# g_norm spread by a small product, chunk 7 stored as halves from two queues, and a new order after chunk 1

## Chip, cores and metric

One core of one Trainium2 chip runs the whole program. The metric is the device time of one execution in microseconds; lower is better.

## What is computed

Two stages, float32 in and out. Linear attention without softmax, then an RMS norm with gains `g_norm`, gives `x` of 4608 rows by 512. A two-layer block with the SoLU activation and a layer norm follows.

```python
# q, k, v: (8, 8, 576, 64)
kv = einsum('bhsd,bhse->bhde', k, v)
o = einsum('bhsd,bhde->bhse', q, kv)
x = o / sqrt(mean(o * o, -1) + 1e-6) * g_norm      # g_norm: (64,)
x = x.transpose(0, 2, 1, 3).reshape(4608, 512)
h = x @ w_in                                       # (512, 1024)
sm = softmax(h)                                    # the sum has 1e-9 added
u = h * sm
ln = (u - mean(u)) / sqrt(var(u) + 1e-6) * g_ln
out = ln @ w_out                                   # (1024, 512)
```

## The kernel before

**Chunks.** The 4608 rows are worked in nine chunks of 512. Chunks 0 to 7 take 512 of the 576 rows of one batch each; chunk 8 takes the 64 rows left over in each of the eight batches (`q_last` gathers them). A name such as `h.5.2.1` is a step, a chunk, and one or two parts of the chunk.

**Steps of a chunk.** POOL issues the loads `q`, `k`, `v`, which cast to bf16. PE makes `kv_mm`; DVE or ACT copies it into `kvd` (steps `kv`). q is transposed, by PE (`qT_mm`, then a copy `qT`) up to chunk 4 and by a transposing DMA on SP (`qT`, line 425) in chunks 5 to 8. `o_mm` (lines 444 and 458) makes the attention output. Up to chunk 5 its norm runs `sq` (ACT squares), `s_mm` (PE, line 508), `ln` and `ex` (ACT, 512 and 516), and `x` (DVE, 528). In chunks 6 to 8 it runs `sq` (ACT), `ssum` (POOL, 473), `sred` (DVE, 478), `rh` (ACT, 484), `rg` (POOL, 489; reads `g_all`, the gains on every partition), `xt` (DVE, 496), and `x`, a transposing DMA on SP (line 500).

Then `h` (PE, lines 583 and 612) is 512 columns into one PSUM bank. Up to chunk 3 follow `exp` (ACT, 590), `u` (DVE, 594), `usq` (squares, mostly POOL, 238), `es` (POOL, 607) and the sums over all of them on PE (`sums`, 694) with `turn`, `stats` (DVE) and `rstd` (ACT). Chunks 4 to 8 have the rows on the partitions: `expt` (ACT, 620), `ut` (DVE, 626), `bn` (DVE statistics, 632), `stats` and `rstd`; and `turnu.c.half` (a transposing DMA on SP, line 648) turns half of `u` into `w`. Half 1 is the output tiles 2 and 3, half 0 the tiles 0 and 1.

`out` (PE, 760) multiplies with `w_out`; `ob` scales a finished tile by `rstd` out of PSUM (DVE 244 or ACT 242) into a buffer, and `store` (SP; in chunk 8 also ACT) writes it to HBM. In chunks 6 and 7 the rows of one tile go to two places in the output, so a store there is two DMAs of 64 partitions each (line 788). In chunk 8 the last tile is made, scaled and stored in two halves of its columns.

**What sets the order.** `ORDER` is written out by hand as a list of steps; the kernel emits them in that order, and each engine runs its own share of the list strictly in order. A step's suffix `:act` puts it on ACT where DVE would be the default (or POOL, for `usq` and `q_last`). `HOME` gives each PSUM tile one of eight banks, used one tile after another. `kept` says how many buffers of a kind there are; `q` has five, so the load of batch 6 waits for the last reader of batch 1, which is `q_last.1`. Semaphores keep what data and buffers require; `needs` in `add` only asserts that the list is in a possible order. A DMA on SP or ACT also waits for one issued eight DMAs earlier on the two. `FILL` puts idle products in front of some early PE steps.

`g_all` is loaded by one DMA on SP that repeats `g_norm` over 128 partitions (line 303). The gains are also among `g_rows` (nine rows of 128, the last one `g_norm` twice), which PE transposes early (`turn_g`) with the identity `eye`.

Of the kernel before, what the change touches and what calls it, by code (L numbers as in the profile page):

```python
# [39 lines left out]
kv.3.1.1:act kv.3.1.0 kv.3.0.2:act kv.3.1.2 ex.2.1.0 x.2.1.0 out.0.1.0 out.0.1.1 kv.3.0.0:act s_mm.2.1.1 ln.2.1.1  # L40
out.0.1.2 out.0.1.3 ob.0.1 usq.1.1 ex.2.1.1 h.2.7.0 x.2.1.1 qT_mm.3.0 qT.3.0:act h.2.5.0 q_last.3:act h.2.4.0 h.2.0.0
h.2.0.1 exp.2.0 q_last.1 h.2.3.0 h.2.6.0 h.2.3.1 exp.2.3 h.2.7.1 qT.3.1 u.2.0 kv_mm.5.0 kv.5.1.0 kv.5.0.1:act q.5.0
exp.2.7 kv.5.0.2:act kv.5.0.0:act h.2.4.1 exp.2.4 store.0.1 kv.5.1.1:act q.6.0 qT.5 u.2.3 u.2.7 kv.5.1.2 h.2.2.0
h.2.2.1 exp.2.2 usq.2.7 h.2.1.0 h.2.1.1 u.2.2 usq.2.0 h.2.6.1 u.2.4 o_mm.3.1 out.1.2.0 usq.2.2 out.1.2.1 exp.2.1
es.2.0 u.2.1 sq.3.1.0 exp.2.6 u.2.6 s_mm.3.1.0 ln.3.1.0 ex.3.1.0 sums.1 turn.1 stats.1 q_last.4 h.2.5.1 sq.3.1.1
out.1.3.0 q_last.2 g_all s_mm.3.1.1 kv_mm.4.0 exp.2.5 x.3.1.0 u.2.5 ln.3.1.1 es.2.1 usq.2.6 kv.4.0.0:act kv.4.0.2
kv.4.1.1 rstd.1 usq.2.5 ob.1.2 kv.4.0.1 ex.3.1.1 x.3.1.1 o_mm.3.0 sq.3.0.0 usq.2.4:act es.2.2 out.1.1.0 usq.2.1
kv.4.1.2:act out.1.3.1 ob.1.3 store.1.3 es.2.3 qT_mm.4.1 qT.4.1 sq.3.0.1 kv.4.1.0:act out.1.0.0 s_mm.3.0.0 ln.3.0.0
ex.3.0.0 out.1.1.1 ob.1.1 s_mm.3.0.1 o_mm.4.1 qT_mm.4.0 ln.3.0.1 ex.3.0.1 x.3.0.0 store.1.2 x.3.0.1 out.1.0.1 qT.4.0
kv_mm.6.0 kv.6.1.1 kv.6.1.0 ob.1.0 sq.4.1.1 store.1.0 kv.6.1.2 kv.6.0.2 s_mm.4.1.1 ln.4.1.1 h.3.5.1 exp.3.5 u.3.5  # L50
sq.4.1.0 h.3.2.1 exp.3.2 u.3.2 usq.3.2 h.3.4.1 exp.3.4 u.3.4 h.3.0.1 kv.6.0.1:act ex.4.1.1 x.4.1.1 exp.3.0 u.3.0
kv.6.0.0 s_mm.4.1.0 ln.4.1.0 h.3.1.1 exp.3.1 usq.3.5 h.3.6.1 kv_mm.7.0 kv.7.1.0 kv.7.0.1:act kv.7.1.2:act usq.2.3
kv.7.0.0:act u.3.1 store.1.1 o_mm.4.0 sq.4.0.0 kv.7.0.2 exp.3.6 kv.7.1.1 h.3.3.1 h.3.7.1 exp.3.3 u.3.3 out.2.2.0
out.2.2.1 es.3.1 sq.4.0.1 s_mm.4.0.1 exp.3.7 es.3.3 u.3.6 ex.4.1.0 x.4.1.0 ln.4.0.1 ex.4.0.1 u.3.7 usq.3.7:act
s_mm.4.0.0 ln.4.0.0 ex.4.0.0 x.4.0.1 qT.6 out.2.0.0 sums.2 out.2.3.0 o_mm.5.0 es.3.2 turn.2 stats.2 rstd.2 x.4.0.0
o_mm.5.1 sq.5.1.0 sq.5.0.1 out.2.0.1 usq.3.4 ob.2.0 sq.5.0.0 out.2.3.1 ob.2.2 store.2.2 ob.2.3 s_mm.5.1.0 ln.5.1.0
ex.5.1.0 x.5.1.0 h.4.1.0 expt.4.1.0 s_mm.5.0.0 ln.5.0.0 sq.5.1.1 out.2.1.0 out.2.1.1 ob.2.1 ex.5.0.0 usq.3.0 es.3.0
x.5.0.0 h.4.3.0 expt.4.3.0 usq.3.3 s_mm.5.0.1 ln.5.0.1 ex.5.0.1 usq.3.6 usq.3.1 sums.3 ut.4.3.0 ut.4.1.0 turn.3
store.2.1 s_mm.5.1.1 h.4.2.0 bn.4.3.0 stats.3 q.7.0 qT.7 x.5.0.1 ln.5.1.1 ex.5.1.1 x.5.1.1 expt.4.2.0 out.3.3.0
ut.4.2.0 bn.4.2.0 rstd.3 out.3.3.1 o_mm.6.0 sq.6.2 sq.6.0 ob.3.3:act ssum.6.0 o_mm.6.1 bn.4.1.0 h.4.2.1 q_last.7  # L60
sq.6.3 expt.4.2.1 ut.4.2.1 sq.6.1 out.3.2.0 out.3.2.1 ob.3.2 h.4.3.1 sred.6.0 expt.4.3.1 h.4.1.1 expt.4.1.1 ssum.6.1
ut.4.3.1 ut.4.1.1 rh.6.0 turnu.4.1 rg.6.0 out.3.0.0 out.3.0.1 ob.3.0:act h.4.0.1 sred.6.1 rg.6.2 o_mm.7.1 rh.6.1
sq.7.1 bn.4.2.1 xt.6.0 xt.6.2 h.4.0.0 expt.4.0.1 expt.4.0.0 rg.6.3 out.3.1.0 sq.7.3 ut.4.0.1 out.3.1.1 ut.4.0.0
ob.3.1:act bn.4.0.0 rg.6.1 xt.6.1 store.3.2 xt.6.3 x.6 turnu.4.0 h.5.2.1 h.5.0.0 ssum.7.1 sred.7.1 expt.5.2.1 ut.5.2.1
expt.5.0.0 ut.5.0.0 h.5.0.1 store.2.0 expt.5.0.1 h.5.1.1 expt.5.1.1 out.4.3.0 h.5.1.0 ut.5.0.1 bn.4.1.1 out.4.3.1
bn.4.3.1 rh.7.1 q_last.6:act expt.5.1.0 rg.7.3 ut.5.1.1 rg.7.1 q_last.5:act qT.8 xt.7.3 xt.7.1 h.5.3.1 expt.5.3.1
bn.4.0.1 o_mm.7.0 ut.5.1.0 ut.5.3.1 out.4.2.0 sq.7.0 sq.7.2 h.5.2.0 expt.5.2.0 out.4.2.1 stats.4 store.3.3 rstd.4
ob.4.3:act h.5.3.0 bn.5.2.1 ssum.7.0 sred.7.0 rh.7.0 rg.7.0 ob.4.2:act ut.5.2.0 bn.5.2.0 bn.5.3.1 turnu.5.0 store.2.3
expt.5.3.0 bn.5.1.0 h.6.2.0 ut.5.3.0 turnu.5.1 expt.6.2.0 ut.6.2.0 h.6.2.1 bn.6.2.0 xt.7.0 h.6.0.0 expt.6.0.0 ut.6.0.0
h.6.1.0 h.6.3.1 expt.6.1.0 expt.6.2.1 ut.6.1.0 expt.6.3.1 h.6.3.0 store.3.1 out.4.0.0 out.4.0.1 ut.6.3.1 expt.6.3.0  # L70
store.4.2 ob.4.0:act rg.7.2 xt.7.2 h.6.0.1 expt.6.0.1 out.5.1.0 ut.6.3.0 o_mm.8.0 o_mm.8.1 bn.5.3.0 ut.6.0.1 bn.6.0.1
bn.5.1.1 sq.8.2 bn.5.0.1 sq.8.0 h.6.1.1 expt.6.1.1 out.5.1.1 sq.8.3 out.5.2.0 out.5.2.1 ssum.8.0 ut.6.2.1 sred.8.0 x.7
sq.8.1 rh.8.0 rg.8.2 ssum.8.1 out.4.1.0 out.4.1.1 ut.6.1.1 turnu.6.0 ob.4.1:act bn.5.0.0 stats.5 xt.8.2 rstd.5 ob.5.2
out.5.0.0 sred.8.1 bn.6.1.0 out.5.0.1 h.7.1.0 expt.7.1.0 rh.8.1 rg.8.0 xt.8.0 ut.7.1.0 bn.6.1.1 h.7.3.0 rg.8.1
bn.6.2.1 xt.8.1 bn.7.1.0 h.7.1.1 out.5.3.0 store.4.3 h.7.0.1 expt.7.1.1 expt.7.3.0 bn.6.3.1 ut.7.3.0 store.5.2
out.5.3.1 h.7.2.0 ob.5.1:act h.7.3.1 rg.8.3 xt.8.3 bn.6.0.0 ob.5.3:act h.7.2.1 expt.7.2.1 turnu.6.1 bn.6.3.0 out.6.2.0
out.6.2.1 ut.7.1.1 bn.7.1.1 store.3.0 stats.6 h.7.0.0 expt.7.3.1 ut.7.3.1 store.4.0 expt.7.0.1 ut.7.0.1 out.6.0.0
out.6.0.1 rstd.6 ob.6.0 store.4.1 x.8 h.8.0.1 h.8.3.0 ob.6.2:act store.5.3 expt.7.0.0 ut.7.2.1 ut.7.0.0 bn.7.2.1
expt.7.2.0 ut.7.2.0 store.6.2 expt.8.3.0 ut.8.3.0 h.8.1.0 h.8.2.0 store.5.1 expt.8.1.0 ut.8.1.0 h.8.3.1 expt.8.3.1
store.6.0 h.8.2.1 h.8.1.1 bn.7.0.0 bn.8.3.0 out.6.3.0 out.6.3.1 out.6.1.0 expt.8.2.0 turnu.7.0 ut.8.2.0 expt.8.2.1  # L80
ut.8.3.1 ut.8.2.1 bn.8.3.1 turnu.7.1 bn.7.0.1 bn.7.3.1 out.6.1.1 h.8.0.0 bn.7.3.0 out.7.1.0 bn.7.2.0 out.7.1.1
turnu.8.1 ob.6.3:act store.6.3 expt.8.1.1 ut.8.1.1 expt.8.0.0 ut.8.0.0 expt.8.0.1 ut.8.0.1 ob.5.0:act store.5.0
bn.8.2.0 turnu.8.0 out.7.0.0 out.7.0.1 ob.6.1:act out.7.2.0 store.6.1 bn.8.1.1 out.7.2.1 stats.7 rstd.7 out.7.3.0
out.7.3.1 bn.8.0.1 ob.7.1 bn.8.1.0 ob.7.2:act store.7.2 out.8.2.0 out.8.2.1 out.8.1.0 out.8.1.1 out.8.0.0 out.8.0.1
# [782 lines left out]
```

## Time and profile before

| what | value |
| --- | --- |
| three runs | 182.73, 183.19 (median), 183.58 us |
| profiled execution | 184.51 us, its span 182.4 us |
| granted TensorE clock, mean | 0.994 |
| ACT, DVE, POOL busy | 74%, 73%, 54% of the span |
| DMA queues, share of 16 engines | loads from POOL 50.0%, the rest 48.6% |
| HBM | 32.54 MB read, 9.44 MB written |

The profile is one execution; the span runs from the first to the last instruction. Matmuls are pipelined and their ends are modelled. A wait is put down to what came last.

### The profile page before, as it was taken

To read this page: it belongs to the slowest core of one execution; us is meant where nothing else is said; L and a number is where in the kernel's file an instruction comes from. 1 tells how busy PE (TensorE), PEld (TensorE's weight loads), DVE (VectorE), ACT (ScalarE), POOL (GpSimd) and SP (SyncE) were. 2 spreads that over 40 slices of the span, in tenths; PEclk is the share of its full clock that TensorE was granted. 3 is DMA by queue.
4 is the path that set the end of the run, shared out by engine and by line. 5 is a ranking of instruction groups with operands and counts; after the bars stand their busy time and mean duration, and the time that the engine had idled before them with its cause. 6 is when DMAs were issued, how large, how long until landed. Compare 5 with 4: busy or idle time off the path is not lost.

```text
span 182.4 us, 5075 instructions
## 1 busy us (share of the span) xinstructions
PE 171.9 (94%) x2057; PEld 83.7 (46%) x2074; DVE 133.5 (73%) x277; ACT 135.6 (74%) x279; POOL 98.0 (54%) x112
## 2 busy tenths in 40 slices
PE   7999899999998999999999999999999999999990
...
GB/s 188 291 213 211 207 313 324 205 210 207 209 207 269 244 207 209 207 193 149 254 131 91 167 127 156 114 205 202 218 167 163 252 262 185 208 140 216 207 239 170
DMA packets 56139, 37.10 MB, mean 203 GB/s; under 512 B 37548, under 2 KB 49332, under 8 KB 56116
## 3 DMA queue, kind: packets, MB, share of 16 engines
q0 software_dynamic: 13552, 16.42, 50.0%
q1 hardware_dynamic: 42132, 19.70, 48.6%
...
q8 instruction: 16, 0.26, 0.5%
...
HBM read 32.54 MB, written 9.44 MB: 230 GB/s over the span
## 4 chain that ended last, share of the span: by engine, by line
PE 56%; DVE 12%; DMA 3%; ACT 1%; issue 1%
PE out_ps L760 22%; PE h_ps L612 17%; PE h_ps L583 8%; DVE bn_sb L632 4%; DVE u_sb L626 4%; DMA w_sb<-u_sb 3%; PE misc_ps L378 2%; PE misc_ps L694 2%; PE s_ps L508 2%; PE o_ps L444 1%; PE misc_ps L416 1%; DVE x_sb L528 1%; PE o_ps L458 1%; DVE w_out_sb L746 1%; DVE usq_sb L496 1%
## 5 line engine op out<-in xcount | busy, mean ns | idle before, releaser
L612 PE MATMUL h_ps<-w_in_sb,x_sb 128*128 128x512 bf16 x153 | 37.0, 379 | 0.8 <-DVE usq_sb L496 0.4
L760 PE MATMUL out_ps<-w_out_sb,w_sb 128*128 128x512 bf16 (+1 forms) x166 | 36.8, 369 | 0.6 <-DMA w_sb<-u_sb 0.3
L238 POOL TENSOR_TENSOR usq_sb<-u_sb 128x512 bf16<-128x512 bf16 x29 | 29.8, 1042 | 9.9 <-PE s_ps L508 6.4
L620 ACT ACTIVATE e_sb<-h_ps,zero_t 128x512 f32<-128x512 f32 x40 | 27.2, 687 | 8.5 <-PE h_ps L612 7.7
L583 PE MATMUL h_ps<-x_sb,w_in_sb 128*128 128x512 bf16 x128 | 30.4, 379 | 1.4 <-DVE x_sb L528 1.4
L760 PE MATMUL out_ps<-w_out_sb,u_sb 128*128 128x512 bf16 x120 | 30.4, 379 | 0.5
L594 DVE TENSOR_TENSOR u_sb<-h_ps,e_sb 128x512 bf16<-128x512 f32 x32 | 20.9, 685 | 8.8 <-ACT e_sb L590 8.7
L626 DVE TENSOR_TENSOR u_sb<-h_ps,e_sb 128x512 bf16<-128x512 f32 x40 | 26.0, 680 | 1.6 <-ACT e_sb L620 1.5
L632 DVE BATCH_NORM_STATS2 bn_sb<-u_sb 128x6 f32<-128x512 bf16 x40 | 25.8, 681 | 0.2
L760 PEld LDWEIGHTS <-w_sb 128*128 128x128 bf16 x168 | 16.3, 98 | 18.7 <-DMA w_sb<-u_sb 0.8
L612 PEld LDWEIGHTS <-x_sb 128*128 128x128 bf16 x160 | 15.4, 98 | 19.0 <-issue 1.2
L528 DVE SCALAR_TENSOR_TENSOR x_sb<-o_ps,g_cols,rst_sb 128x512 bf16<-128x512 f32 x24 | 18.8, 794 | 7.0 <-ACT rst_sb L516 3.8
L590 ACT ACTIVATE e_sb<-h_ps,zero_t 128x512 f32<-128x512 f32 x32 | 20.6, 691 | 4.2 <-PE h_ps L583 4.0
L607 POOL TENSOR_TENSOR es_sb<-e_sb 128x512 bf16<-128x512 f32 x16 | 20.2, 1274 | 2.2 <-ACT e_sb L590 2.2
L583 PEld LDWEIGHTS <-w_in_sb 128*128 128x128 bf16 x128 | 11.9, 98 | 15.8 <-issue 3.2
L760 PEld LDWEIGHTS <-u_sb 128*128 128x128 bf16 x128 | 11.9, 98 | 14.0 <-issue 0.8
L236 ACT ACTIVATE osq_sb<-o_ps,zero_t 128x512 bf16<-128x512 f32 x24 | 15.5, 682 | 3.4 <-PE o_ps L444 3.4
L489 POOL TENSOR_TENSOR lss_sb<-rh_sb,g_all 128x512 f32<-128x512 f32 x12 | 12.3, 1043 | 7.9 <-ACT rh_sb L485 7.9
L473 POOL TENSOR_TENSOR es_sb<-rst_sb 128x512 f32<-128x512 bf16 x6 | 6.9, 1157 | 15.3 <-ACT rst_sb L236 8.9
L512 ACT ACTIVATE lss_sb<-s_ps,eps_t 128x512 f32<-128x512 f32 x20 | 13.6, 685 | 1.7 <-PE s_ps L508 1.6
L516 ACT ACTIVATE rst_sb<-lss_sb,zero_t 128x512 f32<-128x512 f32 x20 | 14.5, 723 | 0.4
L232 DVE CAST kvd<-misc_ps 64x128 bf16<-64x128 f32 (+1 forms) x23 | 6.4, 288 | 9.1 <-PE misc_ps L378 7.7
...
## 6 DMA issues: line engine op xcount, KB each, us to landing
...
```

What stands on the lines that cost most here:

```text
L236: nc.scalar.activation(out=dst, in_=src, func=AF.Square, bias=zero_t[:, :])
L238: on[engine].tensor_tensor(out=dst, in0=src, in1=src, op=MUL)
L528: nc.vector.scalar_tensor_tensor(out=t[:, z, 2 * hf:2 * hf + 2].rearrange("p a (vt w) -> p w (a vt)", w=2), in0=T["o", c, hf, z].rearrange ...
L583: nc.tensor.matmul(bank(("h", c, f), [128, 512])[:, :], w_in_sb[:, dt, f * 128:(f + 1) * 128], T["x", c][:, :, dt, :], start=(dt == 0), st ...
L590: nc.scalar.activation(out=t[:, f % 2, :], in_=T["h", c, f][:, :], func=AF.Exp, bias=zero_t[:, :])
L594: nc.vector.tensor_tensor(out=t[:, f, :], in0=T["h", c, f][:, :], in1=T["e", c, f // 2][:, f % 2, :], op=MUL)
L607: on[engine].tensor_tensor(out=t[:, n, :], in0=e[:, 0, :], in1=e[:, 1, :], op=ADD)
L612: nc.tensor.matmul(bank(("h", c, m, g), [128, 512])[:, :], x[:, NP * (m ^ 2 * odd(c, dt)) + dt, :] if c in TOKA else x[:, m // 2 ^ odd(c, ...
L620: nc.scalar.activation(out=t[:, g, :], in_=T["h", c, m, g][:, :], func=AF.Exp, bias=zero_t[:, :], accum_out=se[:, m, g:g + 1])
L626: nc.vector.tensor_tensor(out=t[:, m, g * 512:(g + 1) * 512], in0=T["h", c, m, g][:, :], in1=T["e", c, m][:, g, :], op=MUL)
L632: nc.vector.bn_stats(out=t[:, m, g, :], in_=T["u", c][:, m, g * 512:(g + 1) * 512])
L760: nc.tensor.matmul(bank(key, [128, d_model])[:, cols], T["w", c][:, m, f, :] if c in TOKS else T["u", c][:, f, m * 128:(m + 1) * 128], w_o ...
```

## The change

The load of `g_all` goes. In its place PE multiplies `g_rows` by the last column of `eye`, repeated 128 times, which leaves `g_norm` on all 128 partitions of a PSUM bank (`spread_g`), and ACT copies it to `g_all`. The stores of chunk 7 become steps of their own, one for each half: half 0 on SP, half 1 on ACT, and the list must have half 1 behind both `turnu.8`. The filler code learns a mark `!`. `ORDER` is the same up to `kv.2.0.2:act` (at about 46 us of the span) and new from there, and `HOME` changes for the tiles after that.

```diff
+    def spread_g(_):
+        nc.tensor.matmul(
+            bank(("misc", "g_all"), [128, D])[:, :], eye[:, NF:NF + 1].to_broadcast([NF + 1, 128]), g_rows[:, 0:D],
+            start=True, stop=True,
+        )
...
     if TOKA:
-        add("g_all", "sp", lambda _: nc.sync.dma_start(g_all[:, :], g_norm[None, :].to_broadcast([128, D])))
+        add("spread_g", "pe", spread_g, ["ident", "gs"], [("misc", "g_all")])
+        add("g_all", "dve|act", lambda e: copy(e, g_all[:, :], T["misc", "g_all"][:, :]), ["spread_g"], [("misc", "g_all")])
...
+    def store_part(engine, c, m, x):
+        rows = out[c * S:c * S + S, :].rearrange("(p j) d -> p j d", j=9)
+        on[engine].dma_start(rows[:, 4 * (m % 2) + m // 2 + 2 * x, :], T[ob_key(c, m)][64 * x:64 * x + 64, :])
...
             for x in range(2):
-                on[engine].dma_start(rows[:, first + 2 * x, :], t[64 * x:64 * x + 64, :])
+                store_part(engine, c, m, x)
...
+            if c in TOKA and c == LAST - 1:
+                for x in range(2):
+                    add(("store", c, m, x), ("sp", "act")[x], lambda _, a=(c, m, x): store_part(("sp", "act")[a[2]], *a),
+                        [("ob", c, m)] + x * [("turnu", LAST, half) for half in range(2)], [ob_key(c, m)])
+                continue
```

The old list in three places, around chunk 2's norm, chunk 4's first steps, and the end:

```
kv.2.0.2:act out.0.3.0 out.0.3.1 out.0.3.2 usq.1.4:act u.1.3 usq.1.3 o_mm.2.0 sums.0 sq.2.0.1 s_mm.2.0.1 es.1.2
sq.2.0.0 v.6.0 s_mm.2.0.0 usq.1.6 ln.2.0.0 ln.2.0.1 ex.2.0.0 turn.0 stats.0 rstd.0 out.0.2.1 out.0.2.2 out.0.2.3
ob.0.2 store.0.2 o_mm.2.1 sq.2.1.0 sq.2.1.1 x.2.0.0 out.0.0.0 out.0.0.1 out.0.0.2 out.0.3.3 ob.0.3:act usq.1.0
store.0.3 out.0.0.3 ob.0.0 store.0.0 ex.2.0.1 s_mm.2.1.0 qT_mm.3.1 kv_mm.3.0 kv.3.0.1 k.7.0 x.2.0.1 ln.2.1.0 v.7.0
kv.3.1.1:act kv.3.1.0 kv.3.0.2:act kv.3.1.2 ex.2.1.0 x.2.1.0 out.0.1.0 out.0.1.1 kv.3.0.0:act s_mm.2.1.1 ln.2.1.1
out.0.1.2 out.0.1.3 ob.0.1 usq.1.1 ex.2.1.1 h.2.7.0 x.2.1.1 qT_mm.3.0 qT.3.0:act h.2.5.0 q_last.3:act h.2.4.0 h.2.0.0
...
bn.8.2.0 turnu.8.0 out.7.0.0 out.7.0.1 ob.6.1:act out.7.2.0 store.6.1 bn.8.1.1 out.7.2.1 stats.7 rstd.7 out.7.3.0
out.7.3.1 bn.8.0.1 ob.7.1 bn.8.1.0 ob.7.2:act store.7.2 out.8.2.0 out.8.2.1 out.8.1.0 out.8.1.1 out.8.0.0 out.8.0.1
out.8.3.0 bn.8.0.0 bn.8.2.1 ob.7.3:act store.7.1 ob.7.0:act stats.8 rstd.8 ob.8.2:act ob.8.1:act store.7.3
store.8.1:act ob.8.0:act store.8.0:act store.7.0 store.8.2 ob.8.3.0:act store.8.3.0 out.8.3.1 ob.8.3.1:act
store.8.3.1:act
```

The new list, around chunk 2's norm, the load of `q.6` to `o_mm.6.1`, chunk 8's norm, and the end:

```
kv.2.0.2:act out.0.3.0 out.0.3.1 out.0.2.1 out.0.2.2 u.1.3 usq.1.3 o_mm.2.0 sq.2.0.1 sq.2.0.0 sums.0 s_mm.2.0.1
usq.1.1 s_mm.2.0.0 ln.2.0.0 ex.2.0.0 turn.0 stats.0 rstd.0 x.2.0.0 out.0.3.2 out.0.3.3 ob.0.3 o_mm.2.1 sq.2.1.0
out.0.2.3 ob.0.2 out.0.0.0 out.0.0.1 out.0.0.2 out.0.0.3 ln.2.0.1 ex.2.0.1 x.2.0.1 s_mm.2.1.0 ln.2.1.0 es.1.2 ob.0.0
v.6.0 out.0.1.0 out.0.1.1 kv_mm.3.0 sq.2.1.1 s_mm.2.1.1 qT_mm.3.0 kv.3.1.1 ex.2.1.0 x.2.1.0 ln.2.1.1 kv.3.0.0
store.0.3 qT_mm.3.1 out.0.1.2 qT.3.0 out.0.1.3 h.2.0.0 ex.2.1.1 usq.1.4:act h.2.2.0 h.2.6.0 x.2.1.1 h.2.0.1 kv.3.1.2
...
usq.2.2 spread_g g_all:act out.1.3.1 x.3.1.1 usq.2.1 es.2.3 qT_mm.4.1 qT.4.1 kv.4.1.2:act kv.4.0.2 s_mm.3.0.1
...
u.3.0 usq.2.5 kv.7.1.1 usq.3.1 s_mm.4.0.0 sq.4.0.1 es.3.3 store.1.3 h.3.3.1 exp.3.3 u.3.3 q_last.1:act out.2.0.1
kv.7.1.2 ln.4.0.0 sums.2 turn.2 store.1.0 kv.7.1.0:act ex.4.0.0 x.4.0.0 s_mm.4.0.1 q.6.0 ln.4.0.1 ex.4.0.1 out.2.2.0
out.2.2.1 stats.2 rstd.2 ob.2.0 o_mm.5.0 sq.5.0.1 ob.2.2 es.3.2 q_last.4 x.4.0.1 o_mm.5.1 sq.5.0.0 qT.6 sq.5.1.1
out.2.3.0 s_mm.5.0.1 ln.5.0.1 out.2.3.1 ob.2.3 usq.3.0 s_mm.5.0.0 q_last.2 s_mm.5.1.1 out.2.1.0 out.2.1.1 ob.2.1
usq.3.4 ln.5.0.0 ex.5.0.1 h.4.2.1 ln.5.1.1 q_last.5 ex.5.0.0 x.5.0.0 usq.3.7 sq.5.1.0 expt.4.2.1 x.5.0.1 h.4.2.0
h.4.1.1 s_mm.5.1.0 ut.4.2.1 h.4.3.1 expt.4.2.0 ut.4.2.0 expt.4.1.1 ut.4.1.1 ex.5.1.1 h.4.3.0 es.3.0 usq.3.2 usq.3.3
x.5.1.1 usq.3.5 es.3.1 sums.3 o_mm.6.1 expt.4.3.1 ut.4.3.1 o_mm.6.0 turn.3 stats.3 expt.4.3.0 ut.4.3.0 ln.5.1.0
ex.5.1.0 x.5.1.0 sq.6.3 h.4.0.0 expt.4.0.0 q.7.0 qT.7 ut.4.0.0 bn.4.1.1 bn.4.3.1 store.2.3 out.3.0.0 out.3.0.1
...
sred.8.1 h.6.3.1 store.3.0 out.5.1.0 expt.6.3.1 expt.6.0.0 ut.6.0.0 out.5.3.0 out.5.3.1 rh.8.1 rg.8.3 bn.6.1.0 xt.8.3
rg.8.1 store.4.2 rstd.5 ob.5.3:act store.5.3 out.5.1.1 xt.8.1 h.7.0.0 expt.7.0.0 h.7.1.0 ob.5.1:act h.7.2.1 ut.6.3.1
store.4.3 turnu.6.1 expt.7.1.0 rg.8.2 xt.8.2 bn.6.3.1 store.5.1 x.8 h.7.0.1 expt.7.0.1 bn.6.2.0 bn.6.0.0 ut.7.0.0
...
ob.6.0:act out.6.3.1 ob.6.3:act ut.8.2.1 ut.8.2.0 store.6.2 expt.8.1.0 ut.8.1.1 bn.7.2.1 h.8.0.1 expt.8.0.1 bn.7.0.0
store.5.0 bn.7.3.1 out.7.1.0 bn.7.1.0 store.6.0 out.7.3.0 ut.8.1.0 out.7.0.0 out.7.3.1 out.7.2.0 out.7.0.1 bn.8.1.1
turnu.8.1 out.7.2.1 ob.6.1:act store.6.1 stats.7 out.7.1.1 rstd.7 ob.7.2:act ob.7.0:act ob.7.1:act ut.8.0.1 out.8.2.0
out.8.2.1 bn.8.2.1 turnu.8.0 out.8.1.0 store.7.1.1 store.7.2.1 bn.8.2.0 store.6.3 out.8.1.1 out.8.0.0 out.8.0.1
bn.8.3.0 ob.7.3 store.7.3.0 bn.8.1.0 bn.8.0.0 bn.8.0.1 stats.8 out.8.3.1 rstd.8 store.7.2.0 store.7.3.1 store.7.0.1
out.8.3.0 ob.8.2 store.8.2:act ob.8.0:act store.8.0:act store.7.0.0 store.7.1.0 ob.8.1 store.8.1 ob.8.3.0:act
store.8.3.0:act ob.8.3.1 store.8.3.1
```

More of the change, by code (lines that the diff above doesn't have):

```diff
@@ L40 @@
[L40 to L84, printed above, removed]
```

78 lines of the change are left out of this document (50 added, 28 removed).

## The prediction

> **What bounds the kernel now.** I read the page first, then the waits, the windows and the chain of waits. The page's rows of engines and slices:
>
> ```profile
> PE 171.9 (94%) x2057; PEld 83.7 (46%) x2074; DVE 133.5 (73%) x277; ACT 135.6 (74%) x279; POOL 98.0 (54%) x112
> ...
> PE   7999899999998999999999999999999999999990
> ```
>
> TensorE is busy in every slice but the first and the last. A busy PE need not be at its pace, so I looked for the pace in the chain:
>
> ```profile
> 57.25 3.45 PE h_ps L583 x16
> ...
> 112.66 3.45 PE h_ps L612 x16
> ...
> 166.79 5.18 DMA w_sb<-u_sb
> 171.97 0.05 issue
> 172.02 5.39 PE out_ps L760 x32
> 177.40 0.02 issue
> 177.43 0.47 ACT v_sb L242
> ```
>
> Sixteen matmuls of 512 columns take 3.45 us early and late: 0.216 us each, nowhere slower where other engines are fuller. So the time is PE's own work, plus PE's gaps, plus what follows the last matmul (177.4 to 182.4, 5.0 us). The waits name the gaps; columns are total, times and longest:
>
> ```profile
> PE h_ps L583 <- DVE x_sb L528: 1.4, 3, 0.6
> ...
> PE h_ps L612 <- DVE usq_sb L496: 0.4, 1, 0.4
> ...
> PE out_ps L760 <- DMA w_sb<-u_sb: 0.3, 1, 0.3
> ```
>
> By the timeline these end at 56.21 (0.61), 140.44 (0.43) and 172.02 (0.34). The windows after 50 us, ten at a time, leave PE idle by 0.67, 0.11, 0.05, 0.05, 0.11, 0.16, 0.05, 0.05, 0.11, 0.49 and 0.05 up to 160, then 0.05 and 0.34: 2.3 us in all. More than that the new order can't take from PE before 177.4; it can add any amount. DVE is next: 29.6 busy of the 30 us from 120 to 150.
>
> The profiled execution took 184.51 us, its span 182.4, so 2.1 lie around the span. The median of the three runs, 183.19, is 1.32 lower. I make the sum against 184.51 and move the median by the same difference. A measurement of this kernel can tell about 0.5%, 0.92 us, from no change.
>
> **g_norm by a product.** Removed: one DMA on SP, issued at 85.02 for 0.57 us; its first reader is POOL's `rg` at 108.43, and SP's next piece started at 85.69 with no engine waiting for it. Worth nothing. Added on PE: one fp32 product of 128x64. The trace has none like it; the nearest rows are the transpose of the gains (195 ns and a 133 ns weight load, also fp32 from 9 rows) below and an fp32 product of 512 columns (429 ns) above. I take 0.2, from 0.1 to 0.4. Added on ACT: a copy of 128x64 from PSUM, like the 0.26 us `kvd` copies; ACT gives away more (below), so nothing. The bank that the product uses is next wanted by `out.1.0`, 1.5 us of PE work later, against 0.26 for the copy: no wait. The `!` that the filler code learns stands in no entry of `FILL`; nothing.
>
> **The order from 46 us on.** The list is the same up to `kv.2.0.2`, so everything before 46 us stays. Instruction counts hardly move: DVE takes 6 more `kvd` copies (0.29 each), and its full-width scalings fall from 15 to 13, plus one half.
>
> The wait at 56.21: chunk 2's `x` came late because ACT, between the squares of chunk 2 and its last `ex`, also did one scaling (`ob.0.3`, 0.69) and three `kvd` copies (0.26 each). In the new order these are DVE's or come later. Walked by rows from the end of `o_mm.2.0`: ACT has 4 squares (0.62 start to start), 8 `ln`/`ex` (0.65) and `rstd` (0.6), 8.3 us, then `x` 0.79, together 9.1; PE has 10.2 us of work until `h.2.0.1`, the product that needs the last `x`. The 0.61 goes; I take -0.6 (from -1.1, with the small losses of 46 to 55, to 0).
>
> The wait at 140.44 was for DVE's `xt.8.2`, which frees the bank of chunk 7's first `h`. DVE's work by rows from 46 us to that point was 76.3 us, PE's 92.8. In the new order that first `h` waits for `xt.8.0`, with 73.9 on DVE and 91.3 on PE, since `ob.3.2` (0.75) has gone to ACT and other work stands later: DVE is 0.9 us better placed than where it lost 0.43. `ob.5.2` and `ob.6.0` go to ACT too, and the last `xt.8` stands 5 us of DVE work earlier. -0.43 (to 0).
>
> The wait at 172.02 was for chunk 8's last transpose: issued at 166.79, 5.18 us, behind `store.6.3` and `store.5.0` on SP, though its data were ready at 165.2. In the new order only `store.6.1` stands between the last two transposes. Counted back from PE's end, `h.8.0.1` ends 13.9 us before it (five output tiles of 1.73, then 5.2 like the last 32 matmuls), so at about 163.5. Then ACT's two `expt` (0.67), `ut.8.1.0` (0.61), `bn` (0.61), the now earlier `stats.7` (0.82) and `ut.8.0.1` (0.61) bring the transpose's issue to 166.8. With 4.4 to 5.2 us it lands at 171.2 to 172.0, and PE gets to `out.8.1` at 172.2. Cover 0.2 to 1.0: -0.34, at worst +0.5.
>
> **Chunk 7's halves and the end.** Each tile was already stored as two halves; SP spent 1.18 us on a pair and its chunk 7 stores ran until 176.2, so `store.8.2` was issued at 176.24 and took 4.4, to 180.6. Now ACT issues four of the eight halves, at 0.35 each as its three stores of chunk 8 show, while it waits for PE anyway (it had 1.40 us free before 173.96). SP is done with them by about 173, and `store.8.2`, now on ACT, can go at 174. Queued behind ACT's issues are `rstd.8`, `ob.8.0` and `ob.8.3.0`; the last begins when PE ends. The last landing becomes that of the last half tile, 177.93 + 2.4 = 180.3. -0.35, from -0.6 to +0.4 (if ACT's store waits on an earlier landing, as it did for 1.04 us at 175.68).
>
> By the Trainium skill (DMA: Bandwidth & Descriptors, Rules for kernel authors), two queues move nothing faster, since both feed the same 16 DMA engines, and save issue time only. The windows agree: DMA share 0.98 and 0.97 from 178 to 180. By that rule alone the -0.35 would be 0 and the sum -0.9.
>
> **New waits.** I counted, from 46 us on, PE's work by rows between a product that starts a chain through ACT, DVE and back and the product that waits for that chain, less the chain's own rows. Under 0.5 us is left at 14 places of the old order and at 15 of the new, none of the new ones in chunks 6 to 8. The old 14 cost what the windows show between 60 and 110, 0.5; I allow +0.3 for what differs (0 to 1).
>
> Sum: 0.2 - 0.6 - 0.43 - 0.34 - 0.35 + 0.3 = -1.2. The profiled execution goes to 183.3, the median to **182.0**. Next late is PE's own work.
>
> **Rivals.** *POOL's queue makes it slower.* `q.6`'s load moves from 60 us to behind `q_last.1` on ACT (its buffer), and POOL's queue stands behind it. Rows: exp 0.69, `q_last` 0.40, the issue 0.80, six squares (1.01 to 1.04), three `es` (1.25 to 1.27), three copies (0.40), handovers 0.15: 13.1 to 13.3 us until `sums.3`. PE's cover from `h.3.3.1` to `sums.3` is 13.3: five h tiles of 0.86, seven halves of out tiles (6.0), `sums.2` 1.25, seven small steps 1.7. Before, POOL ended at 96.67 and `sums.3` began at 97.77: 1.1 to spare. Behind that, `q.7`'s load (6.4, then 5.8 for its transpose) has 12.3 us of PE work before `o_mm.7.1`. It decides once POOL is 0.2 late or the load takes over 6.5; a load with others behind it took 9.5, which makes +3: 185.0. For it: both covers shrank to under 0.3. Against: the DMA share falls from 1.21 (70 to 80 us) to 0.80 and 0.76 (90 to 110), so a lone load may keep its 6.4.
>
> *The gaps only move.* If the tight places cost 1.2 instead of 0.3 and the tail stays: 183.2. For it: 14 tight places against 15. Against: the three named waits each lose their cause.
>
> *PE is not the bound.* Weight loads fill only 46% of the span. If PE had room, DVE, full from 120 to 150, would set the pace, and the three scalings taken off it (0.75 each) are worth 2.25, with the tail 2.6: 180.6. The Trainium skill (Trainium Kernel Development and Optimization, Performance Expectations) reads a trace this way: matmul busy time is a bad metric, weight-load time a good one. By that rule this rival is the likely one; the trace disagrees, with 3.45 us for 16 matmuls whichever engine is full beside them.
>
> **Numbers.** Forecast 0.50 (181.2 to 182.9), gaps only move 0.16, POOL 0.25, DVE 0.09. The range goes from the DVE rival to the POOL rival, 180.7 to 184.9. Faster: two thirds of the forecast's 0.50 and the 0.09 of DVE, 0.42. Same: the rest of the forecast's and the 0.16, 0.33. Slower: 0.25.
>
> **What would show it.** Right: no PE wait for `x_sb` near 56, for `usq_sb` near 140 or for `w_sb` near 172; the last matmul at about 176.5; the last store landing under 3 us after it. Wrong: PE waits near `sums.3` or `o_mm.7.1` (95 to 115 us), with POOL or a `q_sb` load as releaser; ACT idle before `ob.8.0` or `ob.8.3.0` for a store; or PE waits of more than 1 us in sum at places where before had none.

## The result, and the profile after

The changed kernel takes 182.25 us (median; 181.48 to 182.58) against 183.19 (182.73 to 183.72): ratio 0.9939, 95% interval 0.9921 to 0.9958. The forecast was 182.0. The profiled execution took 182.41 us, its span 180.6, at a granted clock of 1.000. That is 2.1 us under the profiled execution of before, more than the 0.94 between the medians, because the one of before was 1.3 over its median.

The page of the changed kernel (engines, then the span in 40 slices):

```profile
PE 170.4 (94%) x2059; PEld 83.7 (46%) x2076; DVE 135.0 (75%) x282; ACT 133.6 (74%) x274; POOL 98.6 (55%) x113
...
PE   7989899899999999999999999999999999999691
```

PE is still the full engine. What is new is the 6 in the third slice from the end. The chain of waits names it (start, us, what):

```profile
122.28 3.45 PE h_ps L619 x16
...
164.89 1.49 DVE bn_sb L639 x3
...
167.09 4.42 DMA w_sb<-u_sb
171.55 5.39 PE out_ps L767 x32
```

Sixteen matmuls still take 3.45 us. The last transpose is issued at 167.09, not 166.79, and the last 32 matmuls, which took 5.39 us from 172.02, take 5.39 from 171.55. So they end at 176.94, 0.46 earlier than before. PE's waits (total, times, longest):

```profile
PE out_ps L767 <- DMA w_sb<-u_sb: 1.5, 1, 1.5
...
PE h_ps L590 <- DVE x_sb L535: 0.8, 2, 0.5
PE out_ps L767 <- issue: 0.5, 2, 0.4
```

The `x_sb` waits that are left all lie before 46 us; the ones near 56 and at 140 (`usq_sb`) are gone. The wait for the last transpose, 0.34 before, is 1.53 now: PE came to it at 170.02 instead of 171.68 and gave 1.2 of the 1.66 us back there. The windows over the tail (start to end, length, PE busy, clock, DMA share, GB/s), of the changed kernel:

```profile
165.00:170.00 5.00, 4.95 (x23) 1.00 0.99 194
170.00:175.00 5.00, 3.47 (x17) 1.00 0.97 260
...
177.00:178.00 1.00, 0.00 (x0) 1.00 0.99 371
178.00:179.00 1.00, 0.00 (x0) 1.00 0.50 176
179.00:180.00 1.00, 0.00 (x0) 1.00 0.01 2
```

The DMA engines run dry at about 178.5, where before they were full until 180 (0.97 from 179 to 180). From the last matmul to the end of the span it is 3.7 us instead of 5.0. Of the span's 1.8 us, then, 1.3 lie behind the last matmul and 0.46 in front of it. Cut at PE's arrival at the last transpose the same 1.8 look otherwise: the arrival is 1.66 earlier (170.02 against 171.68), and PE's wait there and the stretch behind the last matmul are together 5.2 us, against 5.3 before.

### The profile page after: what moved, and what is told of

It is laid out like the page before. It is cut to its first block, busy times and chain, and to the rows that moved or that the text cites. A ratio compares the mean times of both kernels' runs of the same rounds, so it can differ in the third digit from the quotient of the medians.

```text
span 180.6 us, 5089 instructions
## 1 busy us (share of the span) xinstructions
PE 170.4 (94%) x2059; PEld 83.7 (46%) x2076; DVE 135.0 (75%) x282; ACT 133.6 (74%) x274; POOL 98.6 (55%) x113
## 3 DMA queue, kind: packets, MB, share of 16 engines
q10 hardware_dynamic: 752, 1.18, 2.0%
## 4 chain that ended last, share of the span: by engine, by line
PE 76%; DMA 8%; ACT 7%; DVE 5%; issue 2%; POOL 1%; DVEq 0%; ACTq 0%; POOLq 0%
PE out_ps L767 31%; PE h_ps L619 19%; PE h_ps L590 12%; DMA v_sb<-in_v_dram 5%; PE misc_ps L701 3%; ACT e_sb L597 3%; PE s_ps L515 3%; DMA w_sb<-u_sb 2%; PE misc_ps L385 2%; PE o_ps L451 2%; ACT osq_sb L236 2%; DVE x_sb L535 2%; PE misc_ps L423 2%; DVE u_sb L601 1%; PE o_ps L465 1%
## 5 line engine op out<-in xcount | busy, mean ns | idle before, releaser
L767 PE MATMUL out_ps<-w_out_sb,u_sb 128*128 128x512 bf16 x120 | 29.7, 379 | 0.9 <-issue 0.5
L242 ACT ACTIVATE k_sb<-out_ps,rstd_sb 128x512 f32<-128x512 f32 x11 | 7.5, 687 | 7.7 <-PE out_ps L767 7.6
L232 DVE CAST kvd<-misc_ps 64x128 bf16<-64x128 f32 (+1 forms) x29 | 8.1, 286 | 6.8 <-PE misc_ps L385 6.1
```

Of the source, the lines that this page charges most:

```text
L767: nc.tensor.matmul(bank(key, [128, d_model])[:, cols], T["w", c][:, m, f, :] if c in TOKS else T["u", c][:, f, m * 128:(m + 1) * 128], w_o ...
```

## The experiments

All kernels with a name in `a_` are the changed kernel with one edit (two where it says so), those in `b_` the kernel before with one edit (three in `b_all`). Times are compared as ratios to the kernel before, run on the same chip. One percent is 1.83 us, and the ratio of the changed kernel is 0.9939. In the profiles I compare distances from the start of `o_mm.2.0`. Up to there the work is the same in all of them (but for one output step, 0.43 us, between the two lists, and for `a_best`), and it still starts anywhere from 44.9 to 46.2 us.

| kernel | ratio (95%) | `o_mm.2.0` to last matmul | PE's wait for the last transpose | last matmul to end of span |
| --- | --- | --- | --- | --- |
| before | 1 | 131.5 | 0.34 | 5.0 |
| changed | 0.9939 (0.9921 to 0.9958) | 131.1 | 1.53 | 3.7 |
| `a_halves_sp` | 0.9985 (0.9962 to 1.0007) | 131.0 | 1.5 | 4.9 |
| `a_load` | 0.9920 (0.9890 to 0.9950) | 130.4 | 1.1 | 4.0 |
| `a_turn_first` | 0.9898 (0.9864 to 0.9931) | 129.2 | none | 4.3 |
| `a_turn_load` | 0.9920 (0.9894 to 0.9947) | 129.1 | none | 5.1 |
| `a_act_copies` | 0.9973 (0.9944 to 1.0001) | 130.7 | 0.7 | 4.6 |
| `a_pool_late` | 0.9977 (0.9955 to 0.9998) | 131.2 | 0.5 | 4.4 |
| `a_dve_more` | 1.0107 (1.0084 to 1.0130) | 133.9 | none | 3.8 |
| `a_best` | 1.0025 (1.0007 to 1.0042) | 129.4 | none | 4.4 |
| `b_halves` | 0.9970 (0.9949 to 0.9991) | 131.9 | 0.22 | 4.2 |
| `b_dve` | 1.0039 (1.0010 to 1.0069) | not compared | not compared | not compared |
| `b_turn_first` | 0.9998 (0.9974 to 1.0023) | 131.0 | none | 5.2 |
| `b_all` | 0.9985 (0.9962 to 1.0008) | 133.8 | none | 4.3 |

**The halves on two queues, taken back.**

```diff
-  add(("store", c, m, x), ("sp", "act")[x], lambda _, a=(c, m, x): store_part(("sp", "act")[a[2]], *a),
+  add(("store", c, m, x), "sp", lambda _, a=(c, m, x): store_part("sp", *a),
```

> The changed kernel with both halves of every chunk 7 store on SP. Theory A, the halves on ACT shorten the end because SP's issues are what the last stores queue behind: SP gets four more issues of 0.5 to 0.6 us in front of store.8.1 and store.8.3.1, so the stretch from the last matmul to the end of the span goes from 3.66 us to 4.7 or more (before: 5.0), and the time by about +1.0, to 183.2. Rival, the 16 DMA engines are the limit (their share was 0.97 to 0.99 near the end of both kernels) and the queue that issues does not matter: the stretch stays at 3.7 plus or minus 0.2 and the time at 182.3.

Ratio 0.9985, 0.46% (0.84 us) above the changed kernel, and the two intervals do not meet. PE's part is unchanged, the stretch behind the last matmul is 4.9 us. SP's timeline, first of this kernel:

```profile
174.97 1.24 SPq L783 DMA_DIRECT2D out_dram<-k_sb  x2
...
176.26 0.59 SPq L783 DMA_DIRECT2D out_dram<-v_sb  x1
...
176.95 1.34 SPq L794 DMA_DIRECT2D out_dram<-v_sb  x2
```

then of the changed kernel:

```profile
173.06 0.78 SPq L783 DMA_DIRECT2D out_dram<-v_sb  x1
...
174.27 2.68 SPq L794 DMA_DIRECT2D out_dram<-v_sb  x2
```

With all eight halves on it SP is still issuing chunk 7 (L783) at 176.26, and its stores of chunk 8 (L794) start at 176.95 instead of 174.27. The DMA share shows the hole that this leaves:

```profile
174.00:175.00 1.00, 1.00 (x6) 1.00 0.77 248
...
176.00:177.00 1.00, 1.00 (x11) 1.00 0.84 217
...
179.00:180.00 1.00, 0.00 (x0) 1.00 0.99 368
```

Engines that stood at 0.77 and 0.84 while SP was issuing are still full at 180. Theory A is right: the halves on ACT carry the short end. But the short end is not a plain gain over the kernel before. Wait and end together are 6.4 us here, 5.3 before and 5.2 in the changed kernel: in these profiles the new list with all halves on SP is 1.1 us worse at the tail than the old one, and the halves on ACT make that good. In time the new order and the product without them can't be told from the kernel before (0.9985, the interval holds 1).

**The halves alone, in the old list.** The two functions of the change's diff, and in the list

```diff
-out.7.3.1 bn.8.0.1 ob.7.1 bn.8.1.0 ob.7.2:act store.7.2 out.8.2.0
+out.7.3.1 bn.8.0.1 ob.7.1 bn.8.1.0 ob.7.2:act store.7.2.0 store.7.2.1 out.8.2.0
```

and the same for the other three tiles, except that `store.7.0.1` goes behind `store.8.2`.

> The kernel before with nothing but chunk 7's stores as halves on two queues: half 0 on SP, half 1 on ACT, each pair where the whole store stood in the old list. Theory A, that alone shortens the end: SP loses four issues of 0.5 to 0.6 us, store.8.2 goes about 2 us earlier than 176.24, the last store lands 1.6 us after the last matmul instead of 2.8 (the changed kernel's numbers), and the time falls by 0.8 to 1.2, to about 182.2. Rival, the end is short in the changed kernel because its new list also stores chunks 5 and 6 earlier: with the old list the landing stays at 2.4 to 2.8 us behind the last matmul and the time moves by less than 0.4.

Ratio 0.997: 0.55 us, between the two theories. The end is 4.2 us, against 5.0 before and 3.7 in the changed kernel. The last matmul comes 0.4 later after `o_mm.2.0` than before, 0.3 of it a wait for `q.7`'s transpose that the profile before does not have. In the timeline ACT gets stuck on its first half:

```profile
168.87 3.34 ACTq L776 DMA_DIRECT2D out_dram<-k_sb  x1
...
177.00 0.48 ACTq L776 DMA_DIRECT2D out_dram<-k_sb  x1
177.58 0.84 ACT L242 ACTIVATE v_sb<-out_ps,rstd_sb 128x256 f32<-128x256 f32 x2 [0.99 <-DMA out_dram<-k_sb]
```

An issue that takes 0.5 to 0.6 us in the changed kernel held ACT for 3.34 us while the last transpose was under way, and two later issues stood in front of the last scalings, which began 0.99 us late. Why this one took so long the trace doesn't say. By the two medians the halves are worth 0.5 to 0.8 us; whether their places in the list decide how much of it stays is not shown.

**The last transpose ahead of `store.6.1`.**

```diff
-turnu.8.1 out.7.2.1 ob.6.1:act store.6.1 stats.7 out.7.1.1
+turnu.8.1 out.7.2.1 ob.6.1:act stats.7 out.7.1.1
-out.8.2.1 bn.8.2.1 turnu.8.0 out.8.1.0
+out.8.2.1 bn.8.2.1 turnu.8.0 store.6.1 out.8.1.0
```

> The changed kernel with store.6.1 (two issues, 1.87 us on SP) behind turnu.8.0 and not in front of it. Theory A, the 1.53 us wait of PE before out.8.1 is SP's queue: the transpose is issued at 165.1 instead of 167.1, the wait goes to 0.1 or less and the last matmul ends at about 175.5. SP then has 1.2 to 1.9 us more to issue behind it, so of the 1.4 to 1.5 some 0.7 comes back in the end: about 181.5. Rival, the wait is the data's (ut.8.0.1 at 164.6 and a transpose that takes as long as the DMA engines are full): it stays above 1.0 and the time at 182.2. Third, the end takes all of it: no wait, the last matmul at 175.5, and still 182.2.

0.9898, the lowest of all ratios: 181.4 us, 0.75 under the changed kernel (the intervals just overlap). The chain has no transpose in it any more:

```profile
155.30 5.18 PE out_ps L767 x24
160.48 0.86 PE h_ps L619 x4
161.34 3.67 PE out_ps L767 x17
165.01 0.05 issue
165.06 10.13 PE out_ps L767 x54
```

PE runs through to 175.19, and the stretch behind it grows from 3.7 to 4.3. SP's queue was the cause of the wait, and in the profiles the end takes back about 0.6 of the 1.9 us that PE gains.

**The same move in the old list** (`store.6.3` and `store.5.0` behind `turnu.8.0`):

```diff
-turnu.8.1 ob.6.3:act store.6.3 expt.8.1.1 ut.8.1.1 expt.8.0.0 ut.8.0.0 expt.8.0.1 ut.8.0.1 ob.5.0:act store.5.0
-bn.8.2.0 turnu.8.0
+turnu.8.1 ob.6.3:act expt.8.1.1 ut.8.1.1 expt.8.0.0 ut.8.0.0 expt.8.0.1 ut.8.0.1 ob.5.0:act
+bn.8.2.0 turnu.8.0 store.6.3 store.5.0
```

> The kernel before with store.6.3 and store.5.0 (three issues on SP) behind turnu.8.0. Theory A: turnu.8.0 is issued when its data are there (165.3 instead of 166.79), lands by 170.5, and PE's 0.34 us before out.8.1 go. SP's stores behind it start no later than now, so the end keeps its 2.8 us: -0.34, 182.85. Rival, the end is SP's: it issues the same stores and transposes in any order, store.8.2 stays at 176.2 and the time at 183.2.

Nothing: 0.9998. The wait goes and PE ends 0.5 us earlier, but the stretch behind it is 5.2: SP issues `store.8.2` 130.39 us after `o_mm.2.0`, and 130.35 in the kernel before. Where SP issues all of chunk 7, the end belongs to SP; the rival is right.

**g_norm loaded again.**

```diff
-usq.2.2 spread_g g_all:act out.1.3.1
+usq.2.2 g_all out.1.3.1
-        add("spread_g", "pe", spread_g, ["ident", "gs"], [("misc", "g_all")])
-        add("g_all", "dve|act", lambda e: copy(e, g_all[:, :], T["misc", "g_all"][:, :]), ["spread_g"], [("misc", "g_all")])
+        add("g_all", "sp", lambda _: nc.sync.dma_start(g_all[:, :], g_norm[None, :].to_broadcast([128, D])))
```

> The changed kernel with g_all loaded by one DMA on SP again, issued where the product stood. Theory A, the product and the hole after it cost PE 0.45 us near 67 us and SP's queue at the end moves with PE: -0.45, to 181.8, with the wait at the last transpose still 1.5. Rival, SP's queue in front of the last transpose is full by itself and does not move: the 0.45 is given back there, the wait grows to about 2.0 and the time stays at 182.25. Third: a DMA of many small packets in front of other stores costs more than the product, 182.5 or more.

0.9920: 0.35 us under the changed kernel, with overlapping intervals, so the time alone doesn't settle it. The timeline does for PE. The changed kernel:

```profile
66.35 0.41 PE L451 MATMUL o_ps<-qT_sb,kvd 64*64 64x256 bf16 x8
...
67.31 0.43 PE L289 MATMUL misc_ps<-g_rows,eye 9*128 9x64 f32 x2
67.89 0.81 PE L767 MATMUL out_ps<-w_out_sb,u_sb 128*128 128x512 bf16 x3 [0.16 <-issue]
```

and the one with the load:

```profile
65.94 0.41 PE L450 MATMUL o_ps<-qT_sb,kvd 64*64 64x256 bf16 x8
...
67.12 0.81 PE L766 MATMUL out_ps<-w_out_sb,u_sb 128*128 128x512 bf16 x3 [0.16 <-issue]
```

From the `o_ps` matmuls to the `out_ps` ones it is 1.54 us with the product and 1.18 without: the product costs PE 0.36, as two matmuls. The 0.16 behind it is there in both. The wait at the last transpose fell to 1.1, which no theory had: SP's queue moved by more than PE, mostly since `store.6.1` took it 1.31 us instead of 1.87.

**Both together,** `store.6.1` behind `turnu.8.0` and the load:

> The changed kernel with store.6.1 behind turnu.8.0 and with g_all loaded by one DMA on SP again, issued where the product stood. Theory A, the two gains add: the wait at the last transpose (1.53 us in the changed kernel, none with store.6.1 behind it) and the product's 0.36 us both come off PE's time, so ratio 0.9898 - 0.002 = 0.988, about 181.0, with the last matmul 0.3 to 0.4 us earlier after o_mm.2.0 than with store.6.1 moved alone (129.2). Rival, the DMA engines, full from 165 us on, set the end: the last matmul comes earlier, the stretch behind it grows by as much, and the ratio stays at 0.990.

The gains don't add: 0.9920, no better than either alone. The last matmul ends 129.1 us after `o_mm.2.0` (129.2 with the move alone), so the product's 0.36 does not show there, and the stretch behind it is 5.1 instead of 4.3. That the DMA engines are what remains would fit (0.97, 0.93, 0.99 and 1.02 from 165 to 177), but they were as full with the move alone (0.92, 0.95, 1.01 and 1.03), and it was not tried by taking traffic away. What sets the end here is open.

**The product among the steps of the first 20 us,** its copy on DVE, with `store.6.1` behind `turnu.8.0`:

```diff
-usq.2.2 spread_g g_all:act out.1.3.1
+usq.2.2 out.1.3.1
-s_mm.0.0.0 x.0.0.1 v.1.1 ex.0.0.0 warm.8 s_mm.0.1.1 ex.0.1.1
+s_mm.0.0.0 x.0.0.1 v.1.1 ex.0.0.0 spread_g warm.8 s_mm.0.1.1 g_all ex.0.1.1
-misc.g_all:7
+misc.g_all:6
```

> The changed kernel with store.6.1 behind turnu.8.0, and the product spread_g with its copy moved to the first 17 us, where PE runs filler products while it waits for loads. Theory A: the product costs nothing there, and the 0.45 us near 67 come off PE's time with nothing left behind it to swallow them: 0.4 less than the run with store.6.1 behind turnu.8.0 alone (ratio 0.9898), so 0.9875, 181.0. Rival, the end is now set by the DMA engines, full from 165 us on, and not by PE: the time stays at 181.4.

Slower than before, 1.0025, and the fault is in the edit. PE's waits name the line of the product:

```profile
PE misc_ps L289 <- ACT rst_sb L529: 1.8, 1, 1.8
```

I gave the product bank 6, which still held a tile that ACT's `ex.0.0.0` had to read; PE stood 1.8 us for a bank. (`o_mm.2.0` started at 48.5; about 1 us of that is a load of q that came later in this profile.) Against `a_turn_first` the time is up by 2.3. So a stop of PE in the first 20 us was not free, although idle products run there; what the product itself costs at that place this run does not show. Another bank was not tried.

**ACT's three steps of chunk 2's norm back on ACT.**

```diff
-out.0.3.3 ob.0.3 o_mm.2.1
+out.0.3.3 ob.0.3:act o_mm.2.1
-qT_mm.3.0 kv.3.1.1 ex.2.1.0 x.2.1.0 ln.2.1.1 kv.3.0.0
+qT_mm.3.0 kv.3.1.1:act ex.2.1.0 x.2.1.0 ln.2.1.1 kv.3.0.0:act
```

> The changed kernel with ob.0.3, kv.3.1.1 and kv.3.0.0 on ACT again, as before the change (0.69 + 2 x 0.26 = 1.2 us more on ACT between chunk 2's squares and its last ex). Theory A, ACT's load made the waits between 46 and 60 us: PE waits for x_sb before h.2.0.1 come back with 0.1 to 0.7 us, and PE's idle time from 50 to 60 goes from 0.05 to 0.2 or more. Rival, the new places of the steps took the wait away (x.2.0.0 and h.2 start in another order), not ACT's load: idle stays at 0.05 to 0.1. The time: up to +0.6 (182.9), or unchanged if the 1.53 us wait at the last transpose shrinks by as much.

PE's idle time from 50 to 60 goes from 0.05 to 0.51:

```profile
PE s_ps L515 <- ACT lss_sb L519: 0.5, 1, 0.5
```

PE waits, though not for `x_sb` but a step earlier, for a bank that ACT's `ln` had not read yet. The wait at the last transpose shrinks from 1.53 to 0.7. The time, 0.9973, is 0.6 us up, with overlapping intervals. So ACT's load makes PE wait in the new list; that it costs time is not shown.

**The same steps on DVE in the old list,** nothing moved:

```diff
-out.0.3.3 ob.0.3:act
+out.0.3.3 ob.0.3
-kv.3.1.1:act kv.3.1.0 kv.3.0.2:act
+kv.3.1.1 kv.3.1.0 kv.3.0.2
-out.0.1.1 kv.3.0.0:act
+out.0.1.1 kv.3.0.0
```

> The kernel before with ob.0.3 and the copies kv.3.1.1, kv.3.0.0 and kv.3.0.2 on DVE instead of ACT, nothing moved. Theory A, ACT's load made the wait for chunk 2's x: the 0.61 us at 56.21 goes and PE's idle time from 50 to 60 falls from 0.67 to 0.2 or less. Of these 0.5 the wait at the last transpose takes back up to all if SP's queue (store.6.3, store.5.0) does not move: time between -0.5 and 0 (182.7 to 183.2). Rival, the places of the steps made it: idle stays at 0.5 or more and the time at 183.2. Third, DVE is the fuller one there and its own copies come late: slower by 0.2 or more.

The third case: slower, 1.0039 (1.0010 to 1.0069). Its profiled execution took 186.1 us, 1.4 over its median of 184.67, so the wait is read from the next kernel, which has the same edit.

**All three edits in the old list** (`b_halves`, `b_dve` and `b_turn_first` in one):

> The kernel before with the three edits together: chunk 7's halves on two queues, the four small steps of ACT on DVE, and turnu.8.0 in front of store.6.3 and store.5.0; the load of g_norm stays, and so does the rest of the old list. Theory A, these three are what the change is worth, and the last transpose is the part that it lost: 1.0 + 0.5 + 0.34 = 1.8 less, 181.4, which beats the changed kernel's 182.25. Rival, the 200 other moved steps of the new list carry a part (the wait at 140.44 with its 0.43, small gaps): no better than the changed kernel, 182.2 or more.

0.9985: the rival is right, it is no better than the changed kernel. PE's waits in it:

```profile
PE h_ps L583 <- DVE x_sb L528: 2.0, 3, 1.2
PE o_ps L458 <- DMA qT_sb<-q_sb: 1.9, 1, 1.9
```

The wait for `x` doubles, from 0.61 to 1.2, since DVE now has five copies and a scaling in front of it:

```profile
53.13 0.79 DVE L528 SCALAR_TENSOR_TENSOR x_sb<-o_ps,g_cols,rst_sb 128x512 bf16<-128x512 f32 x1
...
53.95 1.09 DVE L232 CAST kvd<-misc_ps 64x128 bf16<-64x128 f32 x4
55.08 0.79 DVE L528 SCALAR_TENSOR_TENSOR x_sb<-o_ps,g_cols,rst_sb 128x512 bf16<-128x512 f32 x1
```

So it isn't ACT's load alone: the new list also spreads DVE's copies over later places. The wait for `usq_sb` at 140 (0.4) is in all four `b_` kernels. The 1.9 for `q.7`'s transpose is taken up below.

**Two steps of POOL behind the load of `q.6`.**

```diff
-usq.2.5 kv.7.1.1 usq.3.1 s_mm.4.0.0 sq.4.0.1 es.3.3 store.1.3
+usq.2.5 kv.7.1.1 s_mm.4.0.0 sq.4.0.1 store.1.3
-s_mm.4.0.1 q.6.0 ln.4.0.1
+s_mm.4.0.1 q.6.0 usq.3.1 es.3.3 ln.4.0.1
```

> The changed kernel with two of POOL's steps (usq.3.1, 1.03 us, and es.3.3, 1.25) moved from in front of the load of q.6 to behind it, so that POOL is 2.3 us later from there on. POOL rival as the prediction has it (it decides once POOL is 0.2 late; a load in company takes over 9 us): PE waits 1.7 us before sums.3, counted from the 0.54 that the trace shows to its start, and again before o_mm.7.1, some +3 us in sum. Theory B, read from the trace of the changed kernel: sums.3 reads the last es only in its third part, 0.9 us after its start, so POOL had 1.45 us to spare and PE waits 0.8; q.7's load and transpose, 12.3 us behind its issue, keep the rest: one wait of 0.8 us near 100, the time between +0.3 and +0.8 (182.6 to 183.1), less if the wait at the last transpose shrinks.

The rows on which theory B rests, of the changed kernel:

```profile
97.48 1.26 POOL L614 TENSOR_TENSOR es_sb<-e_sb 128x512 bf16<-128x512 f32 x1
...
100.19 0.40 PE L701 MATMUL misc_ps<-es_sb,stat_sel 128*32 128x128 bf16 x16
```

and of this kernel, with the one wait for POOL:

```profile
99.42 1.26 POOL L614 TENSOR_TENSOR es_sb<-e_sb 128x512 bf16<-128x512 f32 x1
...
99.89 0.23 PE L701 MATMUL misc_ps<-es_sb,stat_sel 128*32 128x128 bf16 x4
100.73 0.35 PE L701 MATMUL misc_ps<-es_sb,stat_sel 128*32 128x128 bf16 x12 [0.61 <-POOL es_sb L614]
```

PE works through two of the three parts of `sums.3`, and a piece of the third, before it needs the last `es`. It waits 0.61, and `o_mm.7.1` not at all; 0.27 at 121.25 are for a transpose of `u`. The time, 0.9977, is 0.7 us up. Theory B is right.

**Two more scalings on DVE.**

```diff
-turnu.4.1 ob.3.2:act h.4.0.1
+turnu.4.1 ob.3.2 h.4.0.1
-xt.6.3 ob.3.1:act o_mm.7.1
+xt.6.3 ob.3.1 o_mm.7.1
```

> The changed kernel with the scalings ob.3.2 and ob.3.1 back on DVE (1.5 us more on DVE between 105 and 112). Theory A (PE bound, with a counted cover of 0.47 us at chunk 7's first h): PE waits 0.3 to 1.0 us between 112 and 145, above all for DVE's xt of chunk 8 or an x that hangs on it; time +0.3 to +0.8. Rival, DVE sets the pace there: the whole 1.5 us go into the span before 150, and the time rises by 1.2 or more unless the wait at the last transpose takes it. Third: DVE's idle time swallows it, no new wait, 182.3.

Worse than any theory: 1.0107, 3.1 us up for 1.5 us of work moved.

```profile
PE h_ps L619 <- DVE v_sb L244: 1.8, 1, 1.8
PE out_ps L767 <- ACT rstd_sb L724: 1.3, 1, 1.3
PE out_ps L767 <- DVE k_sb L244: 1.2, 1, 1.2
```

PE does not wait for `xt` or `x`, but twice for the bank that the moved scaling (L244) empties, 3.0 us in all between 109.9 and 116.1. By its time alone this is the rival's case (1.2 or more). DVE worked without a break from 108.1 to 116.6 here (in the changed kernel from 108.2 to past 120), so in this stretch it is DVE's queue that sets PE's pace. But PE stood still for 3.0 us where the rival had 1.5, the work that was moved. The third wait, 1.3 near the end, has taken the place of the one for the last transpose.

## Why the prediction was right, and where it wasn't

The time came out within 0.3 us, and two of the three named waits of before went. The terms did less well: two were badly off, and what the one lost the other gave back, so that the sum came so near is partly luck. Up to PE's arrival at the last transpose the forecast had -0.53, behind it -0.69; the two profiles show -1.66 and -0.15.

**The wait at the last transpose, -0.34 forecast, +1.19 measured: wrong in sign, and outside its own bound of +0.5.** The step that failed is the count of SP's queue: "only `store.6.1` stands between the last two transposes". True, but the queue was full before that. SP in the changed kernel (the first row is `store.6.0`, the third `store.6.1`, the others are the transposes):

```profile
159.94 2.84 SPq L783 DMA_DIRECT2D out_dram<-k_sb  x2
162.90 2.10 SPq L655 DMA_TRANSPOSE w_sb<-u_sb  x1
165.11 1.87 SPq L783 DMA_DIRECT2D out_dram<-v_sb  x2
167.09 2.45 SPq L655 DMA_TRANSPOSE w_sb<-u_sb  x1
```

`store.6.0` ended at 162.78, `turnu.8.1` took 2.10 until 165.0, `store.6.1` 1.87 until 166.98 (a pair had been 1.18 to 1.25), while `ut.8.0.1` was ready at 164.6. The issue at 167.09 was forecast at 166.8, but for another reason: that was when the data would be ready, and SP made it. The data and PE both came about 2.2 us earlier than forecast (164.6 for 166.8, and 170.02 for 172.2); the count back from PE's end had taken the old end, 177.4, and not the 176.5 of its own forecast. From the data to PE's arrival there were the 5.4 us of the forecast, and SP used up 2.5 of them. `a_turn_first` shows that SP was all of it.

**The end, -0.35 forecast, -1.34 measured.** The mechanism was right (`a_halves_sp`: 4.9 us without the halves on ACT), the size was not. I let the last half tile take 2.4 us from its issue, as before. But `store.8.3.0`, issued at 177.47, was through by about 179: the DMA share is 0.50 from 178 to 179 and 0.01 behind that. Most of the -1.34 is the other side of the term above. While PE waited its 1.53, the stores went out; where it waits 0.5 or 0.7 with the same list at the end (`a_pool_late`, `a_act_copies`) the end is 4.4 and 4.6, and without that wait (`a_turn_first`) 4.3, so that at equal waits -0.35 was not far off. The two terms were summed as if they were independent, and they are not: PE's end and the DMA engines' end run side by side, and the later one counts.

By the Trainium skill (DMA: Bandwidth & Descriptors, Rules for kernel authors) two queues save issue time only. The runs agree with that sentence, and not with what I made of it, an end that stays: issue time is what the end was short of, 0.84 us of it.

**The wait near 56, -0.6.** It went, with the small losses beside it: PE's idle time from 46 to 60 fell from 0.85 to 0.10, -0.75, within the bounds. The reason given, less on ACT, is half of it: `a_act_copies` brings 0.46 back, but `b_all`, which has the edit of `b_dve`, shows that the same steps put on DVE without moving anything double the wait.

**The wait at 140, -0.43.** Gone as forecast. The cover (time to spare) that I counted on DVE, 0.47 at one place (the 0.9 less the 0.43 lost before), was no guide, though: in `a_dve_more` the banks that a late scaling holds cost PE 3.0 us, at places that I had not counted.

**The product, 0.2 taken, 0.36 measured,** inside 0.1 to 0.4. It runs as two matmuls, and the higher of the two rows was the nearer one.

**New waits, +0.3.** From 60 to 160 PE was idle 1.23 before and 1.11 now. Without the 0.43 at 140 that is 0.80 and 1.11: +0.31. The size is luck, though. The tight chains that I had counted cost nothing that shows: 0.54 of the 1.11 lie between 65 and 68, as two waits (0.38 and 0.16) in which PE waited for nothing that the profile names.

PE arrived at the last transpose 1.66 us earlier than before, where these four terms sum to -0.53. Of this 0.5 lies in front of `o_mm.2.0`, where the change does nothing: that step started 0.08 us earlier, with one output step (0.43) more behind it. Idle time accounts for 0.76 (46 to 60, and 140 to 150, less 60 to 70), and the product took 0.36 the other way. Some 0.7 us are left that do not show as idle time in either trace, whose matmul ends are modelled; where they came from stays open.

**POOL's queue** did not decide, and I had the risk in the wrong kernel. Covers of 0 to 0.3 us were counted to the start of `sums.3`, but the last `es` (done at 98.74) is read by its third part, at 100.19: 1.45 to spare. Behind that, `q.7`'s transpose landed at 110.1, 1.5 before `o_mm.7.1`. In the old list it has hardly any spare time: PE waits for it by 0.3 in `b_halves` and 1.9 in `b_all`.

**PE is not the bound** (180.6): no. DVE has more work now (135.0 busy against 133.5) and the time fell. That weight loads fill 46% says little here: the loads of the `out` matmuls take 98 ns each, beside 216 ns from one matmul to the next, and 98 of 216 is 45%. But the cover beside PE is thin, and from 108 us on DVE has no break either, as `a_dve_more` shows.
